# The last 64 rows of a first MLP product in both row halves of the array, and its bias in the GELU

## The chip, the cores and the metric

The kernel runs on one core of one Trainium2 chip. The metric is device time in microseconds (us) of one execution; lower is better. The engines named below are TensorE (PE; its weight loads are shown as PEld), VectorE (DVE), ScalarE (ACT), GpSimd (POOL) and SyncE (SP), which here only issues transfers (DMAs).

## What is computed

One block with a state-space branch and an MLP branch, on x of shape 1 x 2048 x 448, in bfloat16:

```
xn = layernorm(x)
s  = 2 Re(C h) + Dskip * xn,   h[t] = Lam_bar * h[t-1] + B_bar xn[t]   (448 complex states)
g  = silu( gelu_tanh( layernorm(xn) @ w1 + b1 ) @ w2 + b2 )            (448 -> 1792 -> 448)
out = x + s * g
```

What matters here is the first MLP product, y @ w1 + b1. Its contraction is over 448 = 3 x 128 + 64 rows, so the fourth slice of the contraction fills only half of the 128 rows of the array.

## The kernel before

The 2048 positions are worked on in four groups g of 512 (two blocks b of 256, each of two parities par of 128 rows). The whole program is a list of tasks. A task belongs to one engine, holds one or several instructions, and names what it reads and writes; from these names the waits are derived. The issue order is a fixed list of task numbers, `ORDER`, written into the source; `SECOND` names those tasks that take the second of two possible engines. Each engine works off its tasks strictly in this order, and a task waits for everything that it reads before its first instruction.

The steps that the change and the prediction touch:

- **Loads.** `ldw1` loads w1 in four chunks of 4, 4, 4 and 2 tiles of 128 columns (F tiles): three 128-row slices in one DMA (384 KB; 192 KB for the last chunk), the remaining 64 rows in a second, small DMA (`w1r_0` to `w1r_3`; 64 KB, the last 32 KB). All are issued on SP's queue, with x, B, w2 and C. b1 goes into row 64 of the fourth slice of `w1_sb` (`w1b`); rows 65 to 127 of that slice are set to zero by DVE (L293).
- **Normalised input.** `first_norm` (block 0) and `ln_apply` write xn2 in 512 columns per row: 448 of data, a 1 in column 448 and zeros behind it (memsets L294 and L295). PE transposes (L380 for block 0, L440 for block 1) or DMA transposes (`xt`) turn it into `xn2T`, with four 128-row slices per parity.
- **First product.** For group 0 `mm1_half` (L701) works on one block at a time: 14 tasks (7 pairs j of F tiles, 2 blocks) of 8 matmuls with 256 columns each. For groups 1 to 3 `mm1` (L686) has 7 tasks per group of 8 matmuls with 512 columns each: 2 F tiles times 4 slices, where the fourth slice holds 64 rows of data, the row with b1 against the column of ones, and zeros.
- **GELU.** ACT reads both F tiles of a task (two PSUM banks) in one instruction (L707 of 512 columns, L692 of 1024 columns) and writes `gT`. The PSUM banks are used in turn: three pairs in group 0, two pairs after.
- **Second product** `mm2` (L715), B product `bu` (L616), M0 product (`m0`, L605 and L607), output product `ym` (L747, L750, L753) are the other matmuls.

At the start PE stands in this order: 28 warm-up matmuls (L783), small transposes of the parameters (L456 to L460), transposes of block 0, six `mm1_half` tasks (j = 0 to 5 of block 0; pair j = 0, 1 need chunk 0, j = 2, 3 chunk 1, j = 4, 5 chunk 2, j = 6 chunk 3), the transposes of block 1 (L440), then j = 6 of block 0 and the seven tasks of block 1, then `mm2` of group 0 (L715). On POOL the load of b2 (`b2bc`) waits for `w1r_3`, so that it does not start early.

SP's queue at the start, in the order of issue (one DMA each, KB in brackets):

```
x0p0 (112), x0p1 (112), w1_0 (384), w1r_0 (64), b1 (3.5), x1 (224), w1_1 (384), w1r_1 (64),
w1_2 (384), w1r_2 (64), w1_3 (192), w1r_3 (32), B_re (336), B_re rest (56), B_im (336), B_im rest (56),
w2_0 (448), w2_1 (448), w2_2 (448), w2_3 (224), x2+x3 (448), C_re (392), C_im (336), transposes ...
```

Of the kernel before, what the change touches and what calls it, by code (L numbers as in the profile page):

```python
# [7 lines left out]
ACT = mybir.ActivationFunctionType  # L8
ALU = mybir.AluOpType
BF = dt.bfloat16  # L10
F32 = dt.float32
# [24 lines left out]
class Plan:  # L36
# [33 lines left out]
    def either(self, first, second, reads=(), writes=(), prio=0.0, chain=False):  # L70

        t = self.add(first[0], first[1], reads, writes, chain=chain)
        t.alts.append((second[0], second[1] if isinstance(second[1], list) else [second[1]]))
        return t
# [72 lines left out]
0 9 18 22 10 1 19 23 11 16 15 12 89 2 20 24 3 8 17 21 14 25 13 5 27 26 7 90 6 28 4 91 29 97 46 92 30 98 31 93 99 32 94 47 100 49 95 33 48 50 96 54 104  # L147
101 34 51 102 55 53 103 56 35 63 106 115 52 36 57 107 117 108 64 116 37 109 65 110 38 66 58 119 118 105 39 59 121 120 67 40 123 146 111 122 112 41 125
145 149 124 147 61 45 143 113 62 148 144 60 182 127 73 126 114 42 150 156 129 155 70 154 128 68 153 69 131 157 130 71 72 161 168 133 83 183 158 77 132
74 160 135 75 170 134 76 84 171 137 78 136 79 159 186 81 174 139 169 80 82 138 175 141 86 87 140 85 312 273 88 162 184 310 152 311 142 309 185 314 315  # L150
313 277 316 274 163 317 164 151 165 281 318 166 319 172 278 320 167 321 322 173 285 323 176 279 177 275 280 178 276 180 234 286 282 287 195 43 369 181
235 179 283 192 288 371 284 370 194 373 44 289 372 292 324 193 325 290 375 293 196 327 374 188 328 399 377 198 376 200 201 294 187 204 379 378 199 291
421 202 425 381 419 380 423 402 420 236 424 382 422 197 426 203 427 383 205 237 206 208 207 209 210 387 532 536 431 384 190 220 385 221 391 432 388
224 386 389 211 428 225 212 222 329 392 228 429 395 223 393 189 213 229 226 394 430 437 227 438 214 433 232 230 238 215 231 191 233 216 529 239 533
531 479 535 217 242 243 240 326 480 244 481 241 252 248 218 482 251 249 434 330 250 435 530 219 485 534 331 247 537 390 254 332 396 245 397 246 253
483 486 268 256 257 262 258 333 541 489 263 542 264 484 267 265 266 259 255 260 269 334 261 538 490 539 487 270 540 335 271 398 272 339 295 488 338
340 491 296 297 346 336 492 348 298 345 337 344 497 436 299 347 343 300 302 350 352 353 498 301 354 355 341 543 356 499 342 357 349 400 493 363 351
509 364 358 500 505 359 544 494 360 361 303 545 362 401 304 495 365 305 496 506 501 366 439 507 367 306 368 508 307 405 403 502 503 504 440 406 404
512 408 441 547 548 407 442 409 546 410 412 411 510 443 607 511 444 413 415 445 449 446 549 416 577 447 448 308 450 579 578 453 458 550 580 457 417
581 513 551 451 610 414 452 418 552 459 582 514 455 468 583 456 553 469 470 454 461 471 472 462 554 463 460 464 465 466 585 467 584 473 555 474 587  # L160
586 475 559 556 588 589 476 477 557 558 478 515 560 590 565 566 595 516 564 517 567 518 596 561 597 562 591 569 519 571 598 520 522 568 521 608 592
563 593 609 599 570 594 523 524 572 603 573 574 600 525 575 601 576 604 616 526 605 602 613 606 527 611 528 617 612 620 614 618 615 628 619 621 624
629 622 630 625 623 626 631 627
""".split()]
SECOND = [int(k) for k in """
44 143 144 148 150 168 172 174 178 180 198 200 204 220 230 232 289 290 317 328 402 404 429 434 435 438 511 512 513 538 539 541 542 544 545 607 611 630
# [12 lines left out]
def bass_recurrent_scan__ssm_conv_s5__mixer_channel_mlp__prompt_kernel(  # L179
# [18 lines left out]
    with ExitStack() as es:  # L198
# [22 lines left out]
        De = SB("De", [128, 4, 128])  # L221
        dbc = SB("dbc", [128, D])
# [51 lines left out]
        with nc.Block():  # L274
# [18 lines left out]
            dve(lambda e: e.memset(w1_sb[64:128, 3, :], 0.0), [], ["w1b"], 0.5, S0)  # L293
            dve(lambda e: e.memset(xn2_sb[:].rearrange("p b (r c) -> p (b r) c", r=2)[:, :, D:512], 0.0), [], XM, 0.1, S0)  # L294
            dve(lambda e: e.memset(xn2_sb[:].rearrange("p b (r c) -> p (b r) c", r=2)[:, :, D:D + 1], 1.0), XM, XM, 0.1, S0)  # L295
# [21 lines left out]
            def ldw1(c, prio):  # L317
                a, w = CH[c][0] * 128, CH[c][1] * 128
                ld("sp", w1_sb[:, 0:3, a:a + w], dram_ap(B_w1, a, [[F, 128], [128 * F, 3], [1, w]]), [f"w1_{c}"], 384 * w * 2, prio, dur=0.55)
                ld("sp", w1_sb[0:64, 3, a:a + w], dram_ap(B_w1, 384 * F + a, [[F, 64], [1, w]]), [f"w1r_{c}"], 64 * w * 2, prio)  # L320
# [6 lines left out]
            ld("sp", w1_sb[64:65, 3, :], dram_ap(B_b1, 0, [[F, 1], [1, F]]), ["w1b"], 4000, S1 + 1)  # L327
# [8 lines left out]
            ld("pool", b2bc[:], dram_ap(B_b2, 0, [[0, 128], [1, D]]), ["b2bc"], 114688, -50, reads=["sgn3", "w1r_3"])  # L336
# [28 lines left out]
            def first_norm():  # L365

                for par in range(2):
# [9 lines left out]
                    dve(lambda e, src=src, dst=dst, mean=mean, r1=r1: e.tensor_scalar(dst, src, mean, r1, op0=ALU.subtract, op1=ALU.mult),  # L377
                        [f"x0p{par}", f"r1{par}", f"mv0_{q}", "xm0"], [f"xm0p{par}"], 0.4, 2 * PINNED + par + 0.5)
# [38 lines left out]
            def ln_apply(g, b, par, which, eng, prio):  # L417
                q = par * 2 + b
                dst = xn_sb[:, b, par * D:(par + 1) * D] if which == 0 else xn2_sb[:, b, par * 512:par * 512 + D]
                key = ("xn", "xm")[which] + str(b)  # L420
                rs, nb = lnw[:, g % 2, 2, which, q:q + 1], lnw[:, g % 2, 3, which, q:q + 1]
                src = x_all[:, 2 * g + b, par, :]
                rd = [f"lnw{g % 2}_{b}"] + xk(2 * g + b)
                on = [("dve", lambda e: e.tensor_scalar(dst, src, rs, nb, op0=ALU.mult, op1=ALU.add), 0.4, 0.12),
                      ("act", lambda e: e.activation(dst, src, ACT.Identity, bias=nb, scale=rs), 0.75, 0.2)]
                if eng == "only dve":
                    dve(on[0][1], rd, [key], 0.4, prio)
                else:
                    kb.either(*(on if eng == "dve" else on[::-1]), rd, [key], prio)
# [251 lines left out]

            def mm1(g, j, prio):
                gx, gb = g % 2, g % 2
                b0 = (j % 2) * 2
                rhs = xn2T[:, gx, :, :].rearrange("p (r d) c -> p d r c", r=2)
                fns = [lambda e, k=k, d=d: e.matmul(psum[:, b0 + k, :], w1_sb[:, d, fcol(2 * j + k)],  # L686
                                                    rhs[:, d, :, :], start=(d == 0), stop=(d == 3))
                       for k in range(2) for d in range(4)]
                cs = [chunk[2 * j]]
                pe(fns, [f"xmT{gx}_{b}" for b in range(2)] + [f"w1_{c}" for c in cs] + [f"w1r_{c}" for c in cs] + ["w1b"],  # L690
                   [f"ps{b0}", f"ps{b0 + 1}"], 1.75, prio)
                act(lambda e: e.activation(gT[:, gb, 2 * j:2 * j + 2, :], psum[:, b0:b0 + 2, :], ACT.Gelu_apprx_tanh),  # L692
                    [f"ps{b0}", f"ps{b0 + 1}"] + (WK + WKP if g == 1 else []), [f"gT{gb}_{2 * j + k}_{b}" for k in range(2) for b in range(2)], 1.05, prio - 70, "gelu")

            def mm1_half(j, b, k3, prio):
# [5 lines left out]
                fns = [lambda e, k=k, d=d: e.matmul(psum[:, banks[k], :].rearrange("p (r c) -> p r c", r=2)[:, :, cs],  # L701
                                                    w1_sb[:, d, fcol(2 * j + k)],
                                                    rhs[:, d, :, :], start=(d == 0), stop=(d == 3))
                       for k in range(2) for d in range(4)]
                ws = [chunk[2 * j]]
                pe(fns, (["xmT0p0", "xmT0p1"] if b == 0 else ["xmT0_1"]) + [f"w1_{c}" for c in ws] + [f"w1r_{c}" for c in ws] + ["w1b"], [f"ps{k}" for k in banks], 0.89, prio)
                act(lambda e: e.activation(gT[:, 0, 2 * j:2 * j + 2, :].rearrange("p k (r c) -> p k r c", r=2)[:, :, :, cs],  # L707
                                           psum[:, b0:b0 + 2, :].rearrange("p k (r c) -> p k r c", r=2)[:, :, :, cs], ACT.Gelu_apprx_tanh),
                    [f"ps{k}" for k in banks], [f"gT0_{2 * j}_{b}", f"gT0_{2 * j + 1}_{b}"], 0.6, prio - 70, "gelu")
# [24 lines left out]
            def ym(g, b, par, prio):  # L734
# [9 lines left out]
                def part(c0, c1):  # L744
# [10 lines left out]
                    pe(fns, [f"h{hb}", f"hh{hb}", f"hp{hb}", f"xnT{gx}_{b}"] + rk, [f"ps{bk}"], du, prio + c0 / 1e4)  # L755
# [114 lines left out]
```

## Time and profile before

| what | us |
|---|---|
| time, three runs | 160.48 median (159.83 to 160.59) |
| span of the profiled execution, first to last instruction | 159.2 |
| PE busy | 151.3 (95%) |
| DVE busy | 136.9 (86%) |
| ACT busy | 93.2 (59%) |
| POOL busy | 51.5 (32%) |

The median lies 1.3 us over the span of the profiled execution; this is what lies around the instructions. The TensorE clock was granted at 0.996 over the span. Busy times of PE overlap from one matmul to the next, since a matmul is recorded until its result has left the array; the step from start to start is what counts. A line of a group of instructions gives busy time, the mean of one in ns, then idle time before it and who ended it. A line of the timeline gives start, length, engine, source line, operation and shape; `128*64` is the number of rows and columns of the array that are in use.

### The profile page before, as it was taken

What the parts mean: (1) busy time and instruction counts of PE and PEld (TensorE: products, weight loads), DVE (VectorE), ACT (ScalarE), POOL (GpSimd) and SP (SyncE); (2) the same over time, 40 slices, a digit from 0 to 9 for tenths busy, and PEclk for the clock granted to TensorE, in tenths of its full rate; (3) what the DMA queues carried; (4) which work ended last, traced back from release to release, by engine and by line L of the source; (5) the groups of instructions that cost most, each with busy time, mean ns of one, the idle gap of its engine ahead of it and who ended that gap; (6) DMA issues with size and microseconds to landing.
All of it is one profiled execution on the core that took longest, in us unless ns stands there. A gap on an engine that the chain in (4) does not pass through costs nothing.

```text
span 159.2 us, 2725 instructions
## 1 busy us (share of the span) xinstructions
PE 151.3 (95%) x946; PEld 93.7 (59%) x946; DVE 136.9 (86%) x265; ACT 93.2 (59%) x151; POOL 51.5 (32%) x127
## 2 busy tenths in 40 slices
PE   6959999999999999999999999999989999999990
PEld 6849965565565556566655555576556655555560
DVE  5478969999998799999789999893999599999982
ACT  3839899997779962689835472212456972450200
POOL 5578840007616000038600573302015420060021
PEclk9999999999999999999999999999999999999998
DMA  4999999888980057000210430213401000010032
GB/s 103 260 303 364 315 149 198 139 161 159 276 172 4 0 100 147 0 0 4 48 20 0 120 65 1 57 21 94 116 4 58 0 4 0 0 58 0 0 115 60
DMA packets 31174, 14.70 MB, mean 92 GB/s; under 512 B 24693, under 2 KB 30713, under 8 KB 31162
## 3 DMA queue, kind: packets, MB, share of 16 engines
q1 hardware_dynamic: 30914, 14.26, 39.4%
q0 software_dynamic: 96, 0.23, 0.4%
q8 instruction: 7, 0.11, 0.3%
q10 hardware_dynamic: 152, 0.05, 0.1%
q14 instruction: 5, 0.04, 0.1%
HBM read 6.89 MB, written 1.84 MB: 55 GB/s over the span
## 4 chain that ended last, share of the span: by engine, by line
PE 88%; DMA 7%; SPq 2%; DVE 1%; issue 0%
PE psum L715 27%; PE psum L686 21%; PE psum L616 13%; PE psum L747 12%; PE psum L701 7%; PE psum L750 4%; DMA w_sb<-in_B_w_dram 4%; PE psum L605 3%; DMA xnT<-xn_sb 3%; SPq L84 2%; PE psum L753 1%; PE psum L440 0%; DVE t L756 0%; DVE tmp L759 0%; PE psum L607 0%
## 5 line engine op out<-in xcount | busy, mean ns | idle before, releaser
L715 PE MATMUL psum<-w_sb,gT 128*128 128x448 bf16 x224 | 43.8, 352 | 0.0
L686 PE MATMUL psum<-xn2T,w_sb 128*128 128x512 bf16 x168 | 38.2, 379 | 0.1
L715 PEld LDWEIGHTS psum<-w_sb,gT 128*128 128x128 bf16 x224 | 21.9, 98 | 20.0
L692 ACT ACTIVATE gT<-psum 128x1024 bf16<-128x1024 f32 x21 | 21.4, 1021 | 11.7 <-PE psum L686 11.6
L686 PEld LDWEIGHTS psum<-xn2T,w_sb 128*128 128x128 bf16 x168 | 18.5, 112 | 15.8 <-issue 0.7
L616 PE MATMUL psum<-xnT,BT 128*128 128x256 bf16 x196 | 24.0, 273 | 0.5 <-DMA xnT<-xn_sb 0.5
L616 PEld LDWEIGHTS psum<-xnT,BT 128*128 128x128 bf16 x196 | 19.0, 98 | 5.8 <-DMA xnT<-xn_sb 1.0
L719 ACT ACTIVATE th<-o 128x448 f32<-128x448 f32 x16 | 9.1, 573 | 16.4 <-DVE o L718 16.3
L641 DVE TENSOR_TENSOR_SCAN s_f<-cw,cur,v_sb 128x256 f32<-128x256 f32 x21 | 15.6, 784 | 0.2
L701 PE MATMUL psum<-xn2T,w_sb 128*128 128x256 bf16 x112 | 12.9, 273 | 2.0 <-DMA w_sb<-in_B_w_dram 1.8
L701 PEld LDWEIGHTS psum<-xn2T,w_sb 128*128 128x128 bf16 x112 | 11.8, 112 | 2.8 <-DMA w_sb<-in_B_w_dram 2.0
L620 ACT ACTIVATE u_sb<-psum 128x512 bf16<-128x512 f32 x12 | 7.2, 596 | 10.2 <-PE psum L616 10.0
L731 POOL TENSOR_TENSOR xd<-xn_sb,dbc 128x448 bf16<-128x448 bf16 x4 | 4.8, 1198 | 24.9 <-DVE dbc L339 13.9
L747 PE MATMUL psum<-CZ,h_sb 128*128 128x448 bf16 x56 | 11.9, 352 | 0.0
L756 DVE TENSOR_TENSOR t<-psum,g_sb 128x448 bf16<-128x448 f32 (+2 forms) x17 | 9.9, 589 | 1.7 <-PE psum L750 1.1
L358 DVE BATCH_NORM_STATS2 lnst<-x_all 128x6 f32<-128x448 bf16 x14 | 8.2, 611 | 3.5 <-DMA x_all<-in_A_x_dram 3.5
L720 DVE SCALAR_TENSOR_TENSOR g_sb<-th,o 128x448 bf16<-128x448 f32 x16 | 10.4, 664 | 0.7 <-ACT th L719 0.6
L718 DVE TENSOR_TENSOR o<-psum,b2bc 128x448 f32<-128x448 f32 x16 | 9.7, 614 | 1.3 <-PE psum L715 1.3
L747 PE MATMUL psum<-CQ,h_sb 128*128 128x448 bf16 (+2 forms) x54 | 10.5, 332 | 0.0
L731 POOL TENSOR_TENSOR xr<-xd,g_sb 128x448 f32<-128x448 bf16 x5 | 5.5, 1106 | 14.6 <-DVE tmp L759 14.5
L707 ACT ACTIVATE gT<-psum 128x512 bf16<-128x512 f32 x14 | 8.3, 590 | 3.2 <-PE psum L701 2.9
L731 POOL TENSOR_TENSOR xr<-x_all,xr 128x448 f32<-128x448 bf16 x6 | 6.9, 1156 | 9.2 <-DVE xr L732 9.1
(157 smaller groups left out, 224.8 us busy)
## 6 DMA issues: line engine op xcount, KB each, us to landing
out_dram<-tmp SPq DMA_DIRECT2D x7, 224.0 KB, 2.0
w_sb<-in_B_w_dram SPq DMA_DIRECT2D x3, 448.0 KB, 7.0
x_all<-in_A_x_dram SPq DMA_DIRECT2D x3, 448.0 KB, 4.4
w_sb<-in_B_w_dram SPq DMA_DIRECT2D x3, 384.0 KB, 6.2
gT<-in_A_C_re_dram SPq DMA_DIRECT2D x1, 392.0 KB, 11.6
Bn<-in_A_B_re_dram SPq DMA_DIRECT2D x1, 336.0 KB, 6.5
Bn<-in_A_B_im_dram SPq DMA_DIRECT2D x1, 336.0 KB, 6.4
gT<-in_A_C_im_dram SPq DMA_DIRECT2D x1, 336.0 KB, 12.0
```

What stands on the lines that cost most here:

```text
L616: fns = [lambda e, r=r, m=m, d=d: e.matmul(psum[:, 4, r * NK:(r + 1) * NK], BT[:, m, d, :], xnT[:, gx, d, :], start=(d == 0), stop=(d == 6 ...
L641: dve(lambda e, i=i, ri=ri, init=init: e.tensor_tensor_scan(s_f[:, i, ri, :], col(R2, i).to_broadcast([128, NK]), v_sb[:, i, ri, :], init, ...
L686: fns = [lambda e, k=k, d=d: e.matmul(psum[:, b0 + k, :], w1_sb[:, d, fcol(2 * j + k)], rhs[:, d, :, :], start=(d == 0), stop=(d == 3)) fo ...
L692: act(lambda e: e.activation(gT[:, gb, 2 * j:2 * j + 2, :], psum[:, b0:b0 + 2, :], ACT.Gelu_apprx_tanh), [f"ps{b0}", f"ps{b0 + 1}"] + (WK ...
L701: fns = [lambda e, k=k, d=d: e.matmul(psum[:, banks[k], :].rearrange("p (r c) -> p r c", r=2)[:, :, cs], w1_sb[:, d, fcol(2 * j + k)], rhs ...
L715: fns = [lambda e, fi=fi: e.matmul(psum[:, bk, 0:D], gT[:, gb, fi, q * 128:(q + 1) * 128], w2_sb[:, fi, :], start=(fi == 0), stop=(fi == N ...
L718: dve(lambda e: e.tensor_tensor(o2[:, fb, :], psum[:, bk, 0:D], b2bc[:], ALU.add), [f"ps{bk}", "b2bc"], [f"oo{fb}"], 0.62, prio - 76)
L719: act(lambda e: e.activation(th[:, fb, :], o2[:, fb, :], ACT.Tanh, scale=0.5), [f"oo{fb}"] + (WK + WKP if g == 0 else []), [f"th{fb}"], 0. ...
L720: dve(lambda e: e.scalar_tensor_tensor(out=g_sb[:, gs, :], in0=th[:, fb, :], scalar=1.0, in1=o2[:, fb, :], op0=ALU.add, op1=ALU.mult), [f" ...
L731: kb.either(("pool", lambda e, o=o, i0=i0, i1=i1, op=op: e.tensor_tensor(o, i0, i1, op), 1.37, 0.15), ("dve", lambda e, o=o, i0=i0, i1=i1, ...
L747: fns = [lambda e, k=k: e.matmul(psum[:, bk, c0:c1], h_sb[:, hb, k, k0:k0 + 128], cm[:, k, c0:c1], start=(k == 0), stop=False) for k in ra ...
L756: dve(lambda e: e.tensor_tensor(t3[:, fb, c0:c1], psum[:, bk, c0:c1], g_sb[:, gs, c0:c1], ALU.mult), [f"ps{bk}", f"g{gs}"], [f"t3{fb}_{c0} ...
```

## The change

- The last 64 rows of each w1 chunk are loaded twice, into partitions 0 to 63 (`w1r0_c`) and 64 to 127 (`w1r1_c`) of the fourth slice. Row 64 no longer holds b1, and the zero rows are gone.
- The last 64 columns of xn2 are written twice (columns 384 to 447 and 448 to 511) by a second, 64-column instruction in `first_norm` and in `ln_apply` (13 on DVE, 3 on ACT). After the transpose, both halves of the fourth slice hold the same 64 rows. The memsets L293 to L295 are gone.
- `mm1_fns` issues six full matmuls (two F tiles times three slices), then two matmuls of 64 rows: F tile 2j in rows 0 to 63, F tile 2j+1 in rows 64 to 127. Each F tile has its own PSUM bank.
- b1 is loaded by four DMAs on ACT's queue as columns `b1c` (128 partitions, 4 or 2 values each), turned to float32 by POOL (`b1f`), and given to the GELU as a bias per partition. So each GELU becomes two instructions, one per F tile: 42 of 512 columns in the place of 21 of 1024, and 28 of 256 in the place of 14 of 512.
- `ym` for par = 1 no longer names `xnT` among its reads (it does not use it).

The list `ORDER` has new numbers. Every task that both kernels have keeps its place relative to the others on its engine. The new tasks stand as follows. The four `b1c` loads are the first on ACT's queue, ahead of the four parameter loads and of the first table load. `b1f` is the second instruction of the program on POOL, between the memset of the identity and the operation that finishes the identity. On SP's queue each pair of `w1r` loads stands where its first reader comes up in the list:

```
x0p0, x0p1, w1_0 (384), x1 (224), w1_1 (384), w1_2 (384), w1_3 (192), B_re (336), B_re rest (56),
w1r0_0, w1r1_0 (64 each), B_im (336), B_im rest (56), w2_0 (448), w1r0_1, w1r1_1 (64 each),
w2_1 (448), w2_2 (448), w1r0_2, w1r1_2 (64 each), w2_3 (224), x2+x3 (448), C_re (392),
w1r0_3, w1r1_3 (32 each), C_im (336), transposes ...
```

The load `b2bc` on POOL now waits for `w1r1_3`.

```diff
-            dve(lambda e: e.memset(w1_sb[64:128, 3, :], 0.0), [], ["w1b"], 0.5, S0)
-            dve(lambda e: e.memset(xn2_sb[:].rearrange("p b (r c) -> p (b r) c", r=2)[:, :, D:512], 0.0), [], XM, 0.1, S0)
-            dve(lambda e: e.memset(xn2_sb[:].rearrange("p b (r c) -> p (b r) c", r=2)[:, :, D:D + 1], 1.0), XM, XM, 0.1, S0)
...
-                ld("sp", w1_sb[0:64, 3, a:a + w], dram_ap(B_w1, 384 * F + a, [[F, 64], [1, w]]), [f"w1r_{c}"], 64 * w * 2, prio)
+                for h in range(2):
+                    ld("sp", w1_sb[64 * h:64 * h + 64, 3, a:a + w], dram_ap(B_w1, 384 * F + a, [[F, 64], [1, w]]), [f"w1r{h}_{c}"], 64 * w * 2, prio)
...
-            ld("sp", w1_sb[64:65, 3, :], dram_ap(B_b1, 0, [[F, 1], [1, F]]), ["w1b"], 4000, S1 + 1)
+            for c, (a, n) in enumerate(CH):
+                ld("act", b1c[:, a:a + n], dram_ap(B_b1, a * 128, [[n, 128], [1, n]]), [f"b1c_{c}"], 1000, S1 + 1)
+            pool(lambda e: e.tensor_copy(b1f[:], b1c[:]), [f"b1c_{c}" for c in range(4)], ["b1f"], 0.2, S0)
...
-            ld("pool", b2bc[:], dram_ap(B_b2, 0, [[0, 128], [1, D]]), ["b2bc"], 114688, -50, reads=["sgn3", "w1r_3"])
+            ld("pool", b2bc[:], dram_ap(B_b2, 0, [[0, 128], [1, D]]), ["b2bc"], 114688, -50, reads=["sgn3", "w1r1_3"])
...
+                parts = [(dst, src)] + ([(xn2_sb[:, b, par * 512 + D:par * 512 + 512], src[:, 384:D])] if which else [])
+                on = [("dve", [lambda e, o=o, i=i: e.tensor_scalar(o, i, rs, nb, op0=ALU.mult, op1=ALU.add) for o, i in parts], 0.4, 0.12),
...
+            def mm1_fns(j, outs, rhs):
+                fns = [lambda e, k=k, d=d: e.matmul(outs[k], w1_sb[:, d, fcol(2 * j + k)], rhs[:, d, :, :], start=(d == 0), stop=False)
+                       for k in range(2) for d in range(3)]
+                fns += [lambda e, k=k: e.matmul(outs[k], w1_sb[64 * k:64 * k + 64, 3, fcol(2 * j + k)], rhs[64 * k:64 * k + 64, 3, :, :],
+                                                start=False, stop=True) for k in range(2)]
+                return fns
...
-                act(lambda e: e.activation(gT[:, gb, 2 * j:2 * j + 2, :], psum[:, b0:b0 + 2, :], ACT.Gelu_apprx_tanh),
+                act([lambda e, k=k: e.activation(gT[:, gb, 2 * j + k, :], psum[:, b0 + k, :], ACT.Gelu_apprx_tanh, bias=b1f[:, 2 * j + k:2 * j + k + 1]) for k in range(2)],
```

## The prediction

> **What bounds the kernel now.** The page first: PE is busy nearly all the time, and the chain that ended last runs over PE.
>
> ```profile
> PE 151.3 (95%) x946; PEld 93.7 (59%) x946; DVE 136.9 (86%) x265; ACT 93.2 (59%) x151; POOL 51.5 (32%) x127
> GB/s 103 260 303 364 315 149 198 139 161 159 276 172 4 0 100 147 0 0 4 48 20 0 120 65 1 57 21 94 116 4 58 0 4 0 0 58 0 0 115 60
> PE 88%; DMA 7%; SPq 2%; DVE 1%; issue 0%
> ```
>
> Then the same chain in order of time. Its only long piece off PE is a w1 transfer at the start; from 10.19 us PE works without a break to 112 us, and with one gap of 0.5 us to 154. So a microsecond lost or won on PE after 10 us is one at the end.
>
> ```profile
> 4.20 5.95 DMA w_sb<-in_B_w_dram
> 10.19 3.69 PE psum L701 x32
> 13.88 0.45 PE psum L440 x8
> 14.33 7.09 PE psum L701 x64
> 21.42 10.59 PE psum L715 x56
> ```
>
> The 5.95 us piece is `w1r_1` (the second remainder), issued at 4.20 and landed at 10.15. So the queue is behind its issues by 6 us: what is issued later lands later, whatever its size. The table of DMA issues (KB, us to landing), SP's queue by time, and a DVE wait give more landings:
>
> ```profile
> gT<-in_A_C_re_dram SPq DMA_DIRECT2D x1, 392.0 KB, 11.6
> Bn<-in_A_B_re_dram SPq DMA_DIRECT2D x1, 336.0 KB, 6.5
> w_sb<-in_B_w_dram SPq DMA_DIRECT2D x1, 32.0 KB, 6.0
> ```
> ```profile
> 7.14 1.14 SPq L84 DMA_DIRECT2D Bn<-in_A_B_re_dram  x2
> 12.08 0.47 SPq L84 DMA_DIRECT2D gT<-in_A_C_re_dram  x1
> ```
> ```profile
> 22.22 2.21 DVE L358 BATCH_NORM_STATS2 lnst<-x_all 128x6 f32<-128x448 bf16 x4 [1.28 <-DMA x_all<-in_A_x_dram]
> ```
>
> With the sizes of SP's queue added up, landing against KB issued so far: 10.2 us at 1348 KB, 13.6 (7.14 + 6.5) at 2356, 22.2 (x2+x3) at 4820, 23.7 (12.08 + 11.6) at 5212.
>
> **The change, part 1: when the remainders land.** In the new queue they stand behind other loads, and a first-product task waits for all that it reads before its first matmul, although the remainder is used last. KB issued up to each second copy: 2312, 3280, 4304, 5432 for chunks 0 to 3. By the points above (linear between them; beyond, the last slope) that is 13.5, 16.8, 20.4 and 24.5 us. That is the late end. The early end runs from 13.5 us at the best slice of the page's GB/s line, 364 GB/s or 355 KB/us: 16.2, 19.1, 22.3. Reason for less than the late end: the b2 load and the first DMA transposes, which shared the engines from 13 to 24 us, now themselves wait for `w1r1_3` or stand behind it. I take the middle: 13.5, 16.5, 19.8, 23.4.
>
> PE then: j = 0, 1 at 13.5 to 15.5 (two at 1.0, part 2), wait; j = 2, 3 at 16.5 to 18.5, wait; j = 4, 5 at 19.8 to 21.8; block 1's transposes 0.45, to 22.3; wait; j = 6 at 23.4. Before, it stood at 14.33. Shift: **+9.1 us** (8.0 to 10.2). DVE does not absorb it: its copy of block 1's transposes (L446) stands in front of the tables and B combinations, so DVE too is held until 22.3 and moves by 8. POOL is held at `b2bc` to 23.4 instead of 13.0; behind it stand 8 us of small operations, done by 32, first read by the C combinations, at 39 us before, 48 now. b2bc itself, issued at 23.4 with 6.5 us to landing as before, is there at 30, first needed at the end of the first mm2, at 34; cover 4 us.
>
> Costed at nothing, hidden by the wait to 13.5: the four `b1c` issues on ACT (0.4 each, like SP's 128-row issues) push the parameter loads and the table load to about 2.5; POOL's `b1f` waits for the b1c landing, near 5.1 (2.6 after the issue, as the last parameter load), and holds the identity, for which 28 warm-ups (3.1) and the transposes (2.0, 4.47 to 6.49 before) wait: PE is ready near 10.8. Were the weights in time, this would cost 4.3. The dropped memsets (1.0 us of DVE, before 2.4 us) bring nothing.
>
> **Part 2: the two row halves.** Starts of neighbouring matmuls lie 0.216 us apart at 512 columns (8 in 1.73) and 0.109 at 256. If the halves run side by side, a task loses one such step. But the array changes from full to half use and back. One place shows such a change, the M0 product with 64 columns:
>
> ```profile
> 63.55 1.89 PE L686 MATMUL psum<-xn2T,w_sb 128*128 128x512 bf16 x8
> 65.28 0.93 PE L616 MATMUL psum<-xnT,BT 128*128 128x256 bf16 x7
> 66.04 1.89 PE L686 MATMUL psum<-xn2T,w_sb 128*128 128x512 bf16 x8
> 67.86 1.51 PE L605 MATMUL psum<-CQ,Bn 128*64 128x448 bf16 x7
> 69.21 0.19 PE L607 MATMUL psum<-De,ident 128*64 128x64 bf16 x1
> 69.33 0.94 PE L616 MATMUL psum<-xnT,BT 128*128 128x256 bf16 x7
> ```
>
> Eight L686 take 1.73 to the next start where nothing changes (63.55 to 65.28), 1.82 before the change (66.04 to 67.86): +0.09. The seven L605 behind it take 1.35 against 1.32 in the full-width group at 62.17: +0.03. Back: 0.12 for a 64-column matmul, where a 128-column one took 0.06 (63.49 to 63.55): +0.06 to +0.1. Together 0.18 to 0.22 per round trip, plus about 0.01 between the two starts of the pair. Taken at 0.22 and 0.01: a 512-column task changes by -0.216 + 0.23 = +0.01, a 256-column one by -0.109 + 0.23 = +0.12 (0.89 to 1.01). Of the 14 half tasks the first six are paid in the waits above; 8 x 0.12 + 21 x 0.01 = **+1.2 us**. No row shows *row* halves with real lengths, so bounds: the change free, pair fully parallel, -8 x 0.109 - 21 x 0.216 = -5.4; the pair one after the other and the change paid, 29 x 0.22 = +6.4. I take +1.2, as the M0 row is the nearest. Weight against this a rule of the Trainium skill, page "TensorEngine Tiling (Array Packing)", section "Theoretical Speedup": a contraction of at most 64 rows gains up to 2x by two row tiles. By it alone the sum would be the -5.4 end and the time about 164.5. The same page's "Key Properties" says that a change of tiling mode drains the engine; the M0 row puts 0.2 us on that.
>
> **Part 3: GELU with a bias, one per tile.**
>
> ```profile
> L692 ACT ACTIVATE gT<-psum 128x1024 bf16<-128x1024 f32 x21 | 21.4, 1021 | 11.7 <-PE psum L686 11.6
> L719 ACT ACTIVATE th<-o 128x448 f32<-128x448 f32 x16 | 9.1, 573 | 16.4 <-DVE o L718 16.3
> L425 ACT ACTIVATE xn_sb<-x_all,lnw 128x448 bf16<-128x448 bf16 x11 | 8.3, 755 | 0.8 <-DVE xn_sb L424 0.6
> L707 ACT ACTIVATE gT<-psum 128x512 bf16<-128x512 f32 x14 | 8.3, 590 | 3.2 <-PE psum L701 2.9
> ```
>
> L425 has two per-partition operands (bias, scale), L719 none, at equal width: 182 ns more, so 90 each. L692 against L707: 0.84 ns a column, 160 fixed; hence 0.47 for 256 columns with a bias and 0.68 for 512. Neighbours on ACT start about 0.1 before the other's end. A half task goes from 0.49 to 2 x 0.37 = 0.74, a full one from 0.92 to 1.16: +8.5 us of ACT over the kernel. In the last eight half tasks ACT has 8 x 0.74 and 2.1 of other work, 8.0; PE has 8.1. Where PE works at a full task, 1.73 against 1.16, ACT catches up (11.6 us of idle time at L692 now). At group 1's first tasks ACT is nearly late already; there I put **+0.3 us** (0 to 2). The 13 small DVE operations (0.2 each) lie beside PE; at 0, up to 0.4 where two stand ahead of the xn2 transposes of group 1.
>
> **Sum.** 9.1 + 1.2 + 0.3 = 10.6 us. The profiled span 159.2 becomes 169.8; with the 1.3 around it 171.1, against the median of 160.48.
>
> **The rivals.**
> - *Pair free* (no price for the change of the array). For it: two `vrows` matmuls into column halves (L458) start together; against: the M0 row. 160.5 + 9.1 + 0.3 - 5.4 = 164.5; halfway, 167.5.
> - *Pair in sequence*: the second half waits for the first, or its weight load does. 160.5 + 9.1 + 0.3 + 6.4 = 176.3.
> - *ACT the bound* in the half tasks and at group 1, or a PE clock that falls in the new waits of 1 to 2 us (before, it did not fall in one of 1.8): 2 more, 173.
> - *The other side: the small loads overtake the large ones*, at SP's queue, landing 2.0 us after issue as x0 did. Then PE starts at 10.8 (b1's chain): six tasks and the transposes to 17.3, shift +3.0 and not +9.1: 165.0. It ends below 160.5 only if the pair saves more than 0.13 us per full task as well (3.3 of the 5.4); at the full -5.4, 158.4. Against it: the 32 KB `w1r_3` needed 6.0 us.
>
> **How the numbers follow.** Forecast (late loads, pair near even) 0.62, its own range 169 to 173; pair free or half free 0.15; in sequence 0.10; ACT or clock 0.09; overtaking 0.04, of which 0.02 below. Range 166.0 to 174.5: it takes in the half-free pair and ACT, and leaves out the sequence and most of the overtaking. What a measurement can tell from no change is about 0.5%, 0.8 us. Faster 0.02, same 0.01, slower 0.97.
>
> **What would show it.** First half task near 13.5; PE idle before j = 2, 4 and 6, put down to DMA; j = 6 near 23.4, mm2 near 31.5 (21.42 before). Six full matmuls, then two 64-row ones with starts 0.01 apart, and 0.3 to the next start. GELUs of 0.47 and 0.68. I am wrong if w1's remainders land within 3 us of issue, or if PE has idle time after 35 us.

## The result, and the profile after

| | before | after |
|---|---|---|
| time, median | 160.16 us (159.52 to 160.59, four runs) | 170.51 us (169.98 to 171.49, four runs) |
| ratio, 95% interval | | 1.0665 (1.0612 to 1.0717) |
| span of the profiled execution | 159.2 us | 168.0 us |
| PE, DVE, ACT, POOL busy | 151.3, 136.9, 93.2, 51.5 | 154.0, 138.4, 101.6, 51.7 |

A second set of runs, beside experiments, gave 170.72 us (before: 160.07) and 1.0657 (1.0604 to 1.0711). The change makes the kernel 6.6% slower; 171.1 us had been forecast. Ratios use fast runs alone: one run of e1_again and one of e6, over 1.5% longer than the fastest of their kernel, count in the medians but not in the ratios.

The page of the changed kernel, the same three views: busy time, the GB/s of 40 slices, the shares of the chain that ended last.

```profile
PE 154.0 (92%) x946; PEld 88.4 (53%) x946; DVE 138.4 (82%) x275; ACT 101.6 (60%) x189; POOL 51.7 (31%) x128
...
GB/s 112 300 328 342 301 57 109 136 26 148 155 213 265 31 0 24 183 28 4 2 0 62 55 82 93 0 19 83 123 0 55 0 0 4 0 55 0 0 109 57
...
PE 68%; DVE 11%; SPq 7%; ACT 5%; DMA 4%; issue 2%
```

PE has only 2.7 us more work, while the span is 8.8 longer: some 6 us of the loss are idle time. The chain in order of time shows where it ends. Before, a transfer that landed at 10.15 us started PE's unbroken work; now the chain runs over SP's issues to 14.18, and one of the last remainders of w1 lands at 21.70.

```profile
13.64 0.50 SPq L84
14.18 7.53 DMA w_sb<-in_B_w_dram
21.70 0.09 issue
21.80 0.81 PE psum L689 x6
```

PE's timeline at the start (start, length, line, shape; in brackets the idle time before and who ended it):

```profile
7.58 3.17 PE L792 MATMUL psum<-ident 128*128 128x128 bf16 x28 [7.58 <-POOL mhalf L297]
...
13.47 0.82 PE L689 MATMUL psum<-xn2T,w_sb 128*128 128x256 bf16 x6 [0.33 <-DVE xn2T L387]
...
15.47 0.85 PE L689 MATMUL psum<-xn2T,w_sb 128*128 128x256 bf16 x6
...
17.68 0.82 PE L689 MATMUL psum<-xn2T,w_sb 128*128 128x256 bf16 x6
...
21.80 0.81 PE L689 MATMUL psum<-xn2T,w_sb 128*128 128x256 bf16 x6 [1.50 <-DMA w_sb<-in_B_w_dram]
22.54 0.28 PE L691 MATMUL psum<-xn2T,w_sb 64*128 64x256 bf16 x2
22.76 0.85 PE L689 MATMUL psum<-xn2T,w_sb 128*128 128x256 bf16 x6
```

The rows are the warm-ups (1.42 before), j = 0, 2, 4 and 6 of block 0, and the first task of block 1. Only j = 6 waits long for a load. The first half task was not held by its weights, which had landed at 11.70, but by the chain that starts at b1. POOL's timeline shows its head:

```profile
0.79 0.20 POOL L279 MEMSET ident<- 128x128 bf16 x1 [0.29 <-POOLq L864]
6.99 0.20 POOL L329 CAST b1f<-b1c 128x14 f32<-128x14 bf16 x1 [6.00 <-DMA b1c<-in_B_b_dram]
7.24 0.29 POOL L280 TENSOR_SCALAR_AFFINE_SELECT ident<-ident 128x128 bf16<-128x128 bf16 x1
```

POOL stood 6.00 us at `b1f`, with the identity, and so the warm-ups and transposes, behind it. The last `b1c` load landed at 6.83, 4.6 us after its issue.

Two full tasks later in the program, and ACT's GELU groups:

```profile
84.31 0.41 PE L691 MATMUL psum<-xn2T,w_sb 64*128 64x512 bf16 x2
84.65 1.49 PE L689 MATMUL psum<-xn2T,w_sb 128*128 128x512 bf16 x6
86.07 0.41 PE L691 MATMUL psum<-xn2T,w_sb 64*128 64x512 bf16 x2
86.41 1.70 PE L620 MATMUL psum<-xnT,BT 128*128 128x256 bf16 x14
```
```profile
L703 ACT ACTIVATE gT<-psum,b1f 128x512 bf16<-128x512 f32 x42 | 26.4, 684 | 8.5 <-PE psum L691 8.4
...
L715 ACT ACTIVATE gT<-psum,b1f 128x256 bf16<-128x256 f32 x28 | 11.5, 472 | 2.8 <-PE psum L691 2.7
```

The single records of this trace say what the rows sum up. The two 64-row matmuls start 4 ns apart. From the last full matmul to the pair it is 0.311 us, from the pair to the next full matmul 0.337, where a plain step is 0.216. The first step between full matmuls behind a pair takes 0.244. So the pair saves one step of 0.216 and pays 0.095 for going in, 0.121 for going out and 0.028 at the first step after: 0.24 to 0.25 in all. A full task that follows another takes 1.76 us in place of 1.73.

To follow the loss along the program, compare the start of the same PE instruction in two traces. PE's lag behind the profiled execution of before, in us (b0 and b1 are the blocks of group 0):

| kernel | j=0 b0 | j=6 b0 | mm2 | group 1, first task | after group 1 | end |
|---|---|---|---|---|---|---|
| after | 6.95 | 7.63 | 8.55 | 8.37 | 8.85 | 8.59 |
| after, second set | 6.45 | 8.22 | 9.15 | 9.01 | 9.44 | 9.18 |
| e2 w1 early | 5.65 | 4.51 | 5.48 | 5.51 | 5.84 | 5.64 |
| e3 both early | 1.66 | 1.94 | 2.92 | 2.66 | 3.27 | 3.06 |
| e4 = e3, no pairs | 2.06 | 0.98 | 1.80 | 1.53 | 2.62 | 2.46 |
| e7 = e4, one GELU, no bias | 1.60 | 1.16 | 1.22 | 0.93 | 1.21 | 0.75 |
| e8 = e7, b1c away | 0.35 | 0.00 | 0.13 | 1.34 | 1.35 | 0.89 |

Between the last two columns the lag falls by 0.2 to 0.5. At 117 us it falls by 0.6 to 0.7, where the kernel before waited 0.51 for a DMA transpose of `xnT` and the changed ones do not; 0.2 to 0.5 of that is lost again near 134 us. The profiled execution of before was also a long one (159.2; seven later runs in one call had spans of 157.8 to 159.3), so the times of one call are the better measure of a total, and the lags that of a place.

### The profile page after: what moved, and what is told of

It is laid out like the page before. It is cut to its first block, busy times and chain, and to the rows that moved or that the text cites. A ratio compares the mean times of both kernels' runs of the same rounds, so it can differ in the third digit from the quotient of the medians.

```text
span 168.0 us, 2787 instructions
## 1 busy us (share of the span) xinstructions
PE 154.0 (92%) x946; PEld 88.4 (53%) x946; DVE 138.4 (82%) x275; ACT 101.6 (60%) x189; POOL 51.7 (31%) x128
## 4 chain that ended last, share of the span: by engine, by line
PE 68%; DVE 11%; SPq 7%; ACT 5%; DMA 4%; issue 2%
PE psum L724 21%; PE psum L689 15%; PE psum L756 11%; PE psum L620 9%; SPq L84 7%; DMA w_sb<-in_B_w_dram 4%; PE psum L691 4%; PE psum L759 4%; PE psum L609 3%; DVE s_f L645 2%; ACT gT L703 1%; DVE xn_sb L428 1%; DVE tmp L768 1%; DVE o L727 1%; ACT s_b L649 1%
## 5 line engine op out<-in xcount | busy, mean ns | idle before, releaser
L689 PE MATMUL psum<-xn2T,w_sb 128*128 128x512 bf16 (+1 forms) x210 | 42.6, 339 | 2.4 <-DMA w_sb<-in_B_w_dram 1.5
L724 PEld LDWEIGHTS psum<-w_sb,gT 128*128 128x128 bf16 x224 | 21.8, 98 | 20.1
L703 ACT ACTIVATE gT<-psum,b1f 128x512 bf16<-128x512 f32 x42 | 26.4, 684 | 8.5 <-PE psum L691 8.4
L689 PEld LDWEIGHTS psum<-xn2T,w_sb 128*128 128x128 bf16 x210 | 21.1, 113 | 15.8 <-issue 3.5
L620 PEld LDWEIGHTS psum<-xnT,BT 128*128 128x128 bf16 x196 | 18.3, 98 | 5.1 <-issue 2.2
L715 ACT ACTIVATE gT<-psum,b1f 128x256 bf16<-128x256 f32 x28 | 11.5, 472 | 2.8 <-PE psum L691 2.7
L691 PE MATMUL psum<-xn2T,w_sb 64*128 64x512 bf16 (+1 forms) x70 | 12.7, 359 | 0.0
L428 DVE TENSOR_SCALAR xn_sb<-x_all,lnw 128x448 bf16<-128x448 bf16 (+1 forms) x30 | 10.9, 398 | 0.6
L792 PE MATMUL psum<-ident 128*128 128x128 bf16 x28 | 3.2, 313 | 7.6 <-POOL mhalf L297 7.6
L691 PEld LDWEIGHTS psum<-xn2T,w_sb 64*128 64x128 bf16 x70 | 3.9, 107 | 11.4 <-issue 11.4
```

What stands on the lines that cost most here:

```text
L428: on = [("dve", [lambda e, o=o, i=i: e.tensor_scalar(o, i, rs, nb, op0=ALU.mult, op1=ALU.add) for o, i in parts], 0.4, 0.12), ("act", [lam ...
L620: fns = [lambda e, r=r, m=m, d=d: e.matmul(psum[:, 4, r * NK:(r + 1) * NK], BT[:, m, d, :], xnT[:, gx, d, :], start=(d == 0), stop=(d == 6 ...
L689: fns = [lambda e, k=k, d=d: e.matmul(outs[k], w1_sb[:, d, fcol(2 * j + k)], rhs[:, d, :, :], start=(d == 0), stop=False) for k in range(2 ...
L691: fns += [lambda e, k=k: e.matmul(outs[k], w1_sb[64 * k:64 * k + 64, 3, fcol(2 * j + k)], rhs[64 * k:64 * k + 64, 3, :, :], start=False, s ...
L703: act([lambda e, k=k: e.activation(gT[:, gb, 2 * j + k, :], psum[:, b0 + k, :], ACT.Gelu_apprx_tanh, bias=b1f[:, 2 * j + k:2 * j + k + 1]) ...
L715: act([lambda e, k=k: e.activation(gT[:, 0, 2 * j + k, :].rearrange("p (r c) -> p r c", r=2)[:, :, cs], psum[:, b0 + k, :].rearrange("p (r ...
```

## The experiments

Two theories of the loss stood at first. One is that of the prediction: the late w1 remainders alone make it, with small fixed prices for pair and GELU. The other is that of nested waits: the remainders, the b1 chain and smaller delays lie inside one another at the start, so that undoing one brings out the next. (The letters of the theories in an expectation hold for that run alone.) Ratios are to the kernel before in the same call.

**e1 and e1_again: only b1's chain moved later.** SP's queue stays as in the changed kernel.

```diff
 ACT queue:  - b1c x4, vrows x4, table load ...
             + vrows x4, b1c x4, table load ...
 POOL:       - identity memset, b1f, identity ...
             + identity memset, identity, ..., b1f just before the first GELU
```

> The changed kernel with b1's steps moved back at the start: the four b1c loads stand behind the four parameter loads on ACT's queue (still ahead of the first table load), and POOL's b1f stands just ahead of the first GELU, so the identity no longer waits for b1c. The w1 remainders stay late. In the profile of the changed kernel the first half task began at 13.47 us, on a DVE copy and not on a w1 load (the first remainders landed at 11.7), while task j = 6 began at 21.80, just after its remainders at 21.70. Theory A, the late loads set the end: tasks 0 to 5 start earlier, but j = 6 still waits for 21.7, so the time stays at 170.5 (within 0.5). Theory B, the b1 chain sets the end: the first task moves from 13.5 to about 8 and the time falls by up to 6, to about 165.

> e1 once more (b1's chain moved later and nothing else), for whether its last remainder of w1 always lands later than in the changed kernel (23.2 us there, 21.7 and 22.3 in two executions of the changed kernel). Theory A, it is the order of the loads: landing near 23.2 again and a ratio of 1.072 or more. Rival B, executions differ by this much on their own: a landing between 21.5 and 22.5 and a ratio of 1.066 within 0.005, that is, moving b1's chain alone changes nothing, since the last remainder sets the start of j = 6 in both.

Measured: 171.94 us, ratio 1.0771 (1.0683 to 1.0858), and the second time 171.15 us, 1.0672 (1.0599 to 1.0745); the changed kernel itself had 1.0657. The last remainder landed at 23.19, then at 22.28; in the two traces of the changed kernel at 21.70 and 22.29. So two executions of one kernel differ by 0.6 to 0.9 us in this landing, and moving b1 alone changes nothing that can be told: j = 6 waits for that landing either way. Right in e1_again was rival B. PE's timeline of e1_again holds a surprise:

```profile
7.34 0.44 PE L385 MATMUL psum<-ident 128*128 128x128 bf16 x5
11.93 1.44 PE L689 MATMUL psum<-xn2T,w_sb 128*128 128x256 bf16 x6 [4.14 <-DMA w_sb<-in_B_w_dram]
13.30 0.40 PE L691 MATMUL psum<-xn2T,w_sb 64*128 64x256 bf16 x2
13.63 1.47 PE L689 MATMUL psum<-xn2T,w_sb 128*128 128x256 bf16 x6
...
15.38 0.84 PE L689 MATMUL psum<-xn2T,w_sb 128*128 128x256 bf16 x6
```

Transposes are done early, then PE waits 4.14 us for `w1r1_0`, and the first half tasks take 1.7 us each in place of 1.0, at a granted clock of 0.50. It cost nothing here, since j = 6 waited anyway.

**e2: only the w1 remainders moved.** Both copies stand right behind their chunk in SP's queue; b1 as in the changed kernel.

```diff
 SP queue:  w1_0,
+           w1r0_0, w1r1_0,
            x1, w1_1,
+           w1r0_1, w1r1_1,
            w1_2, ... B_re, B_re rest,
-           w1r0_0, w1r1_0,
            B_im ...
```

> The changed kernel with both copies of each w1 remainder right behind their chunk on SP's queue (as in the kernel before, plus the second copy); b1's steps stay as changed. Theory A alone (late loads, everything else hidden, as forecast): the shift at the start goes, 170.5 - 7.6 = 162.9 or a little more. Theory C, two waits stand one behind the other, the b1 chain (13.3 us) under the late loads (21.7 us): the first task stays at 13.4 and six tasks, the transposes and j = 6 follow without a wait, j = 6 at 20.1 instead of 21.8, so only 1.6 to 1.7 us come back: 168.8.

Measured: 166.97 us, ratio 1.0438 (1.0368 to 1.0507). Every wait for w1 is gone, and the whole wait sits at the warm-ups, as PE's list of waits shows:

```profile
PE psum L792 <- POOL mhalf L297: 6.4, 1, 6.4
PE psum L689 <- ACT gT L703: 0.3, 1, 0.3
```

Over before of its own call the kernel is 7.4 us longer, where the changed one is 10.65 longer: the move gave back 3.2, and j = 0 still lags by 5.65, now through b1's chain alone. With the remainders as the only cause it would have been 162.9, with nested waits I had put 168.8: these are right in kind, and the move was worth more than I had put. About 1.1 us of it need not be the move's: the last `b1c` load landed at 5.70 in this trace, in that of the changed kernel at 6.83.

**e3: both moves.**

> Both moves together. Theory C (two nested waits): the first task at about 8, j = 2 at 10.7 (second chunk's remainders, 0.4 later than before for the two second copies), then PE without a break: 12 half tasks of 1.01 and the transposes, the second product from 23.3 (21.42 before). With 0.3 to 0.5 for the rest: 160.2 + 1.9 + 0.4 = 162.5 (161.5 to 163.3). If something else than these two orders cost the 10 us, the time stays over 166.

Measured: 164.42 us, ratio 1.029 (1.0218 to 1.0362). The two moves together are worth 5.8 us; alone they gave 0 and 3.2. That is what nested waits look like. But 4.9 us of loss remain where I expected 2.3 (3.1 at most). PE's timeline:

```profile
6.71 0.40 PE L383 MATMUL psum<-ident,xn_sb 128*128 128x128 bf16 x4 [1.62 <-DVE xn_sb L380]
...
9.57 1.47 PE L689 MATMUL psum<-xn2T,w_sb 128*128 128x256 bf16 x6
```

The first transposes come at 6.71 (4.93 before), and the second half task again takes 1.74 us. Two things not in my sum: the next experiments take them apart.

**e4: e3 without pairs.** Four full matmuls per F tile, lower half of the slice zero, no second small copy of xn2; GELU and bias as changed.

```diff
-  6 full matmuls, then the two 64-row matmuls
+  for k in range(2) for d in range(4): matmul(outs[k], w1_sb[:, d, ...], rhs[:, d], start=(d == 0), stop=(d == 3))
```

> As the one before (both moves), but without the row halves: the lower 64 rows of the fourth slice of xn2 are zero, the second 64-column copies are gone, and each F tile has four full matmuls; b1 stays a bias, one GELU per tile. Forecast for the pair (0.12 per half task, 0.01 to 0.03 per full one): 12 x 0.12 + 21 x 0.025 = 2.0 faster than the one before, so about 160.6. Rival, the pair saves its step in the 512-column tasks: no faster than the one before, or slower. What is left over 160.2 is the price of the GELUs and of the second copies of the loads: 0.4 expected, 2 or more if ACT is the bound in the half tasks.

Measured: 164.02 us, ratio 1.0258 (1.0186 to 1.033): 0.4 less than e3, where I expected 2. From j = 6 to mm2 e3's lag grows by 0.98 (8 half tasks at 0.12, as in the sum). In e4 it grows by 0.82 as well, but for another reason, and at group 1 it grows by another 1.1:

```profile
PE psum L383 <- DVE xn_sb L380: 1.4, 1, 1.4
PE psum L689 <- ACT gT L700: 1.3, 2, 0.9
PE psum L689 <- ACT gT L712: 0.4, 1, 0.4
```

Without pairs PE is faster than ACT with its two GELUs, and waits for it. The price of the pair lies over the price of the GELUs, not beside it.

**e5: pairs of neighbouring tasks adjoin.** In every second task the pair comes first, so in 12 places the array changes once for two tasks.

```diff
-  return fns + pair
+  return pair + fns if first else fns + pair     # first: every second task
```

> Beside e3 (ratio 1.029). In every second first-product task the pair of 64-row matmuls now comes first instead of last, so that in 12 places (7 between half tasks, 5 between full tasks) two pairs stand next to each other and the array changes to half use and back once for two tasks. Theory A, the price is that of the change (0.095 us into a pair, 0.12 out of it, as measured in the changed kernel): pair to pair takes one plain step, 0.11 or 0.22, and each of the 12 places saves 0.2, 2.5 us of PE; ACT, which has two GELUs per task, gives some of it back in the half tasks, so 1.3 us (0.8 to 2.5) less at the end: ratio 1.021 (1.013 to 1.024). Rival B, the price belongs to a 64-row matmul wherever it stands (its weight load, its drain): pair to pair takes 0.3 as well, and the ratio stays 1.029 within 0.004.

Measured: 164.36 us, ratio 1.0248 (1.0203 to 1.0293), against 1.029 of e3. Theory A said 1.021, B 1.029: the time alone does not tell them apart. PE's timeline in group 1 does:

```profile
39.83 1.46 PE L689 MATMUL psum<-xn2T,w_sb 128*128 128x512 bf16 x6 [1.11 <-ACT gT L703]
41.23 0.62 PE L691 MATMUL psum<-xn2T,w_sb 64*128 64x512 bf16 x4
41.78 2.78 PE L689 MATMUL psum<-xn2T,w_sb 128*128 128x512 bf16 x12
44.50 0.80 PE L691 MATMUL psum<-xn2T,w_sb 64*128 64x512 bf16 x4
45.23 1.05 PE L689 MATMUL psum<-xn2T,w_sb 128*128 128x512 bf16 x4
```

Two adjoining pairs take 0.55 us (41.23 to 41.78): 0.24 from pair to pair, which is near a plain step, and 0.31 for the second pair with the way out. The two tasks from 39.83 on take 3.27 us in the single records, against 3.46 for two of before and 3.51 for two with separate pairs. So the price is that of the change of the array, not of a 64-row matmul. But PE had waited 1.11 for ACT just before, and the second two pairs take 0.73 (44.50 to 45.23) in place of 0.55. In the half tasks the gain arrives: from j = 6 to mm2 the lag grows by 0.62 in place of e3's 0.98. In group 1 it does not: there the lag grows by 0.88, in e3 by 0.61.

**e6: both 64-row matmuls in the same rows.**

```diff
-  w1_sb[64*k:64*k+64, 3, ...], rhs[64*k:64*k+64, 3]
+  w1_sb[0:64, 3, ...], rhs[0:64, 3]
```

> Beside e3: both 64-row matmuls of a pair now use rows 0 to 63 (weights and data of the first copy; the result is the same). Theory A, the two row halves work side by side and this alone saves the second step: the two starts lie 0.22 apart (0.11 in a half task) instead of 0.004, 21 x 0.216 + 14 x 0.109 = 6.1 us more, about 5 to 6 at the end since some half tasks wait for ACT anyway: ratio 1.062 to 1.068. Rival B, that the step is saved by something else than the halves, such as matmuls of 64 rows taking half the time: ratio 1.029 as in e3, or 1.045 where each of the two takes half a step.

Measured: 170.25 us, ratio 1.0619 (1.0568 to 1.0669), at the lower end of what theory A gave. It holds by the starts of the single matmuls: the two row halves do run side by side, and only the different halves make them. In a task of group 1:

```profile
43.96 1.49 PE L689 MATMUL psum<-xn2T,w_sb 128*128 128x512 bf16 x6
45.38 0.62 PE L691 MATMUL psum<-xn2T,w_sb 64*128 64x512 bf16 x2
```

The second of the two starts 0.243 after the first instead of 0.004, and the task takes 1.97 us (43.96 to 45.93) instead of 1.75.

**e7: e4 with one GELU for both F tiles.** It has no bias, so b1 is left out of the computation.

```diff
-  act([... activation(gT[2j+k], psum[b0+k], Gelu, bias=b1f[...]) for k in range(2)])
+  act(activation(gT[2j:2j+2], psum[b0:b0+2], Gelu))
```

> As e4 (no pairs, four whole matmuls per F tile, both moves), but the GELU is one instruction for both F tiles and has no bias, so b1 is left out of the computation. Theory A: two GELUs with a bias per task are what holds PE up in e4 (its waits for ACT at half tasks, at the third task of group 1 and near 134 us: 0.8, 0.9 and 0.4 us): these go, PE's lag behind the kernel before stays at the 1.0 us of the first 22 us, and the time falls by 1.4 us (1.0 to 2.0) against e4: ratio 1.017 (1.013 to 1.020). Rival B: PE waits there because ACT and DVE started later, whatever the GELU: ratio 1.026 as in e4, within 0.004.

Measured: 162.18 us, ratio 1.013 (1.008 to 1.0181). PE's waits for ACT are gone, and its lag stays at 0.9 to 1.2 from j = 6 to the end of group 1. The difference to e4 is 1.4 us (lag after group 1) to 2.4 (times over before, 4.5 and 2.1). Two things can make it, and no run here parts them: the two GELUs, and the wait of the first of them for `b1f`, which e7 drops as well. In e4, and by the same 2.3 us in e3, e5 and e9, that wait held the table load ahead of the first GELU:

```profile
9.62 1.28 ACT L712 ACT_TABLE_LOAD   x1 [2.27 <-POOL b1f L330]
```

In e7 this table load began at 7.38. So ACT was late with the first GELU, and not only slower at each. What is left shows in ACT's timeline:

```profile
2.20 1.94 ACTq L84 DMA_DIRECT2D b1c<-in_B_b_dram  x4
4.18 1.28 ACT L285 ACT_TABLE_LOAD   x1 [4.18 <-issue]
5.49 0.29 ACT L377 ACTIVATE lnw<-lnmv,eps 128x1 f32<-128x1 f32 x1
```

Before, the table load began at 2.21 and the first normalisation at 3.80. The four issues of `b1c` hold both back by 2.0 and 1.7 us, and the transposes behind them.

**e8: e7 with the b1c loads in the middle of the program.**

```diff
-  ACT queue: vrows x4, b1c x4, table load
+  ACT queue: vrows x4, table load, ..., b1c x4 before a GELU of group 2
```

> As e7 (no pairs, one GELU without bias), but the four b1c loads and b1f, which nothing reads there, stand in the middle of the program instead of ahead of ACT's table load. What then remains of the change is the second copy of w1's last rows in SP's queue. Theory A: the 1.2 us that e7 still lags at mm2 come from the four issues (1.94 us on ACT's queue, table load at 4.18 instead of 2.21, first transposes 1.6 us later and at a fallen PE clock); these go, and the ratio falls from 1.013 to 1.002 (0.998 to 1.006). Rival B: the lag comes from the longer SP queue (4 x 64 KB in the place of w1's single remainders before j = 2): the ratio stays at 1.010 to 1.014.

Measured: 162.34 us, ratio 1.0137 (1.0084 to 1.0189): no gain. Rival B had the number (1.010 to 1.014) by luck, since the lag ahead of j = 2 that was to make it is not there. Up to mm2 theory A is right; PE's lag is 0.00 at j = 6 and 0.13 at mm2. Then a third layer comes out, in the chain that ended last:

```profile
13.77 9.79 DMA x_all<-in_A_x_dram
23.59 2.21 DVE lnst L361 x4
...
30.64 4.31 DMA xn2T<-xn_sb
35.00 12.28 PE psum L689 x56
```

The load of x2 and x3, behind the second copies in SP's queue, landed at 23.56 (22.20 before); DVE's statistics follow it, then the transposes of group 1, and PE waits for these until 35.00 (group 1 began at 33.66 before): 0.64 us, after 0.52 at mm2 for DVE. In e7 that load was late too (22.98), under a PE that lagged anyway. How much of this is the 224 KB of second copies and how much the scatter of executions stays open: the landing lay at 21.8 to 23.8 in the eight traces with this order of SP's queue (e2 to e9), in three of them earlier than before, so the scatter alone is as large as the delay.

**e9: the change whole, both moves, adjoining pairs, b1 in two loads.**

```diff
-  for c, (a, n) in enumerate(CH): ld("act", b1c[:, a:a + n], ...)
+  ld("act", b1c[:, 0:12], ...[[4, 128], [512, 3], [1, 4]])
+  ld("act", b1c[:, 12:14], ...[[2, 128], [1, 2]])
```

> As e5 (the change whole, with both moves and adjoining pairs), but b1 is loaded by two DMAs on ACT's queue instead of four. Theory A of e8: half of the 1.94 us goes, so the transposes come 0.97 us earlier, and since nothing else is late there the end comes 0.6 to 1.0 us earlier: ratio 1.020 (1.017 to 1.022) against 1.025. Rival B: w1's second chunk (landed at 10.4 to 12) is what counts, and the gain is nested behind it: 1.025 within 0.003.

Measured: 162.64 us, ratio 1.0166 (1.0125 to 1.0207), the best form of the change that I ran, and still slower than before: slightly better than theory A had it. j = 6 came 0.9 us earlier than in e5, as two issues fewer promise; group 1's transposes (0.8 us of wait) took part of it back.

## Why the prediction was right, and where it was not

- *The sum.* 171.1 us against 170.5 and 170.7. Part of that is luck: the growth of the span was forecast at 10.6 and was 8.8; the time around it was taken at 1.3 and was 2.1 to 2.4. Later runs of before had 1.8 around theirs, so subtracting the profiled span from the median of other executions was the mis-sized term there.
- *Late remainders, +9.1.* The mechanism was right, one landing was decisive (j = 6), and the size was off: 7.6 in the first trace, below the bounds of 8.0 to 10.2, and 8.2 in the second, just inside. The landings were taken at 13.5, 16.5, 19.8 and 23.4; they were 11.70, 14.61, 17.59 and 21.70, 1.7 to 2.2 us earlier and earlier even than the early end (22.3 for the last; 22.29 in the second trace). The step that failed is the curve of landing against KB. It was read from a queue in which x1 took from 5.67 to 8.57; in the changed queue x1 took from 5.72 to 6.64. So x1 took 2.0 us less, about as much as every landing came earlier: that time belonged to that place, not to the KB. Why it was lost there was not tested. One candidate is the b1 load into a single row, which stands ahead of x1 in the queue of before and is gone from the changed one; scatter is another, since in e2 to e9, without that load, x1 landed 0.65 to 2.1 us after the load ahead of it.
- *PE idle before j = 2, 4 and 6.* Wrong for j = 2, and 0.2 us for j = 4. The tasks in between had been late already, for the reason of the next point.
- *b1's chain, hidden, PE ready at 10.8.* Wrong. The load was taken at 2.6 us to landing and needed 4.6, and the warm-ups and transposes behind it took 5.9 instead of 5.1 (7.58 to 13.47). The copy of the transposes ended at 13.2; a part of the 0.8 us more is PE's clock, recorded as full only from 12.86 on in this trace (a row of four transposes took 0.61, before 0.40). And j = 0 stood at 13.5 as forecast, for another reason. At the end it was hidden, as costed: e1 shows that nothing comes back without it. The 4.3 given as its price with the weights in time is of the size that e2 and e3 show between them, 2.6 us in time and 4.0 at j = 0.
- *Row halves, +1.2.* Right in kind, and the price a little low: 0.22 was taken for the round trip and 0.246 measured, because the longer first step behind a change was counted for one of the two changes and comes at both. 0.01 between the starts was 0.004, the half task 1.01. The full task was +0.03 (1.758) behind another and +0.00 (1.730) between B products, over the 21 about +0.3 where 0.2 was forecast. From j = 6 to mm2 the lag grew by 0.92 to 0.98 for 8 half tasks. The M0 product with its 64 columns was a good stand-in for 64 rows. The Trainium skill, page "TensorEngine Tiling (Array Packing)", section "Theoretical Speedup", promises up to 2x; e6 shows that the halves do run in parallel, and the records that the step won per task is lost again at the two changes.
- *GELU.* 0.47 and 0.68 were measured to the digit. +0.3 at group 1 was 0.3; another 0.35 at 134 us (an ACT wait in group 3) was not foreseen, nor were the 0.6 to 0.7 us regained at 117. The forecast called the cost small because ACT has idle time. That is true only under the slower pairs: with the pairs gone, e4 and e7 show 1.4 to 2.4 us for the GELUs and the late `b1f` together.
- *The rivals.* Pair free is refuted by the 0.311 and 0.337 around the pair, pair in sequence by the 4 ns and by e6. Overtaking is refuted: the remainders took 5.5 to 7.8 us from issue to landing, and 5.8 to 8.4 in the second trace. A falling clock did not occur in the changed kernel (0.995), but did in e1, e3, e6 and e7, all with b1's chain moved later. A slip: half-way between the free pair and the forecast pair is 167.8 and not 167.5; nothing else rests on it.
- *POOL and DVE held, nothing late behind them.* Right. Idle time of PE after 35 us had been named as a sign of being wrong; 0.5 us of it came, for ACT, inside the +0.3 (0 to 2) put for it.

What stays open: why x1 was slow in the queue of before, how much the second copies delay x2 and x3, how the price of the two GELUs and that of the late `b1f` divide, and what decides over the clock at the start.

## What to carry to other kernels

At the start of a kernel waits lie inside one another: undoing one of two causes gave 0 or 3.2 us, undoing both 5.8, and under them lay the issue of four tiny loads on ACT's queue and then a later x load. So price each delay with the others gone before calling it hidden. With one pair between two changes, splitting the array by rows lost 0.03 us per task at 512 columns and 0.12 at 256 in this kernel. With two pairs next to each other it saved PE 0.18 per two tasks at 512 columns, yet no kernel here came out faster than before.

## What the hardware showed that I had not expected

- **Going to half the rows and back costs a little more than a step of 512 columns.** 0.095 us in, 0.121 out and 0.028 at the first step after, against 0.216. In the records of the changed kernel the 64-row weights are loaded only 0.31 us after the start of the last full matmul (48.70 to 49.01), and the pair starts 5 ns later; between full matmuls the next weight load begins 2 ns after a matmul's start. Two 64-row matmuls in the same rows follow one another at 0.243, as the first step behind a change does, a little over the plain 0.216.
- **The clock fell after a short wait, with a delay.** In e3, PE paused 1.6 us before 6.71. Two of the windows behind it (window, length, PE busy, PEld, DVE, ACT, POOL, granted clock, DMA share, GB/s):

```profile
8.00:10.00 2.00, 1.82 (x11) 1.05 (x12) 1.83 (x7) 0.37 (x1) 1.68 (x10) 0.64 1.10 285
10.00:12.00 2.00, 2.00 (x11) 1.06 (x10) 1.73 (x12) 1.99 (x5) 0.41 (x3) 0.51 1.12 245
```

  The clock was 1.00 until 8.55 us and then 0.50 to 11.97, while PE was at work; e1_again has 0.50 from 8.60 to 15.43. Before, a pause of 1.8 us at 8.4 to 10.2 was followed by 1.00. The pause alone therefore does not decide it; what else does was not tested. The clock at the start also differs from one execution to the next: e3 and e5 have the same program up to the transposes at 6.71, and a row of four of them took 0.40 us in e3 and 0.61 in e5. In e5 steps were as long as that until 10.6 us, in e4 and e9 until 9.7 and 9.9. So a part of the loss ahead of j = 6 in e3, e4, e5 and e9 is the clock's, and not that of the order of loads.
- **Tiny loads are not quick.** Loads of 8 bytes per partition, 1 KB in all, and half of that for the last, took 0.47 us each on average to issue on ACT's queue and up to 5.6 us to land (3.54 to 9.18 in e4).
